# Block-sparse attention feeding a mixture of experts: the third chunk of keys is multiplied with V one step later, and the first group's queries alternate between the column halves of TensorE

## The chip, the core and the metric

The kernel runs on one core of one Trainium2 chip. The core has five engines with queues of their own: TensorE (PE, its weight loads are shown as PEld), VectorE (DVE), ScalarE (ACT), GpSimd (POOL) and SyncE (SP), which here issues most of the DMA transfers. Engines wait for one another through semaphores. Matrix products are written to PSUM banks, everything else lives in SBUF. The metric is the device time of one execution in microseconds (us).

## What is computed

The first half is BigBird attention: batch 4, 8 heads, 768 positions, head size 64, in blocks of 32 positions. A query block sees its own block and its two neighbours, the first and the last block, and three blocks drawn at random for it; the first and the last query block see everything. The second half is a mixture of 8 experts: a gate picks one expert for each of the 3072 rows, and the row goes through that expert's two layers.

```python
mask = np.abs(blk_i - blk_j) <= window
mask = mask | (blk_i == 0) | (blk_j == 0) | (blk_i == n_blocks - 1) | (blk_j == n_blocks - 1)
for qb in range(n_blocks):
    for kb in sampled_blocks[qb]:
        mask[qb * block:(qb + 1) * block, kb * block:(kb + 1) * block] = True
scores = np.where(mask, scores, -1000000000.0)
...
return np.matmul(attn, v).astype(np.float32)
...
x = np.ascontiguousarray(attn_out.transpose(0, 2, 1, 3)).reshape(B * S, H * D)
...
logits = x @ w_gate
expert_idx = np.argmax(logits, axis=1)
...
h = np.maximum(x_sorted[lo:hi] @ w1[e], 0.0)
y_sorted[lo:hi] = h @ w2[e]
return (gate_w[:, None] * y).astype(np.float32)
```

## The kernel before

**Steps.** Attention is a list of 48 steps, worked through by the loop over `steps` in the main program: 4 batches, in each 6 groups of queries, in each 2 halves (two pairs of heads, `pr`, a half). Step i has i % 12 as its place in the batch; even steps are a group's half 0, odd steps its half 1. A group is 128 queries in two tiles of 64 (`ti` 0 and 1). The first group of each batch (GL, places 0 and 1) is different: 64 ordinary queries, and the 64 queries of the first and the last block, which see all 768 keys.

**Keys and values.** An ordinary tile of queries has three chunks of 128 keys. For chunk 0 the rows of V are put in place by copies; for chunks 1 and 2 most of them are gathered from `v_rows` in DRAM by indirect DMAs on POOL (`fetch_values`, L525), four for a group, into `around`, which holds two groups. The gather for the second tile's chunk 2 is issued at the beginning of the group's own half 0, the other three during the group before. POOL's tiny copies into `paced` (`not_before`, L539) hold a gather back until another engine has got to a certain place.

**A step on each engine.** The order on all engines is written by hand. PE in step i: scores of step i (L349, L357), a transpose of 12 pieces of the next batch's K or Q (`turn`, L178; the staging tile is filled by SP, `fill_stage`, L140), in odd steps the transposes of a finished group (`turn_out`, L469), then the products with V of step i - 1 (`product`, L386), and in odd steps that finished group's gate logits (L492). ACT takes the exponentials of the scores (L362) into a ring of 7 tiles `ea`; DVE multiplies by the mask (L368, L372) and, when the products of step i - 1 are done, divides by the sums (`divide`, L445 to L451). When a group's half 1 is divided, SP stores its rows (L457). SP also loads V for the next batch (L161), writes it to `v_rows` (L170), and stores the gate weights (L517, L519). Each of SP's transfers is issued in the program's order.

**Halves of the array.** A product has 64 queries as columns of the stationary operand, so it uses one half of TensorE's columns, and its result lands in partitions 0 to 63 or 64 to 127 of a PSUM bank. `op[ti * D : (ti + 1) * D, ...]` in `product` picks the half by `ti`. Each product shows as two records in the trace, since the data is float32. An ordinary step has 24 products (48 records), tile 0 and tile 1 in turns. In the first group, `attend_last` takes 18 products for each pair: 12 that alternate between the halves, then 6 with `ti` 1 alone. In the first batch the 48 products of the 64 all-seeing queries are computed ahead of step 0 (`attend_all`), all with `ti` 1, and steps 1 and 2 then have 12 products each, all with `ti` 0.

**Banks.** The pool `ps_o` has two banks. One holds the results of one step; the logits are written beside them into the bank of step i - 1, and `divide` reads the bank and frees it.

**After attention** the experts run tile by tile: layer 1 (L1138), layer 2 (L1152). Their 2 MB weight transfers wait on SP for PE to free a buffer (L1085, L1088).

## Time and profile before

| what | value |
|---|---|
| median of three runs | 640.93 us (637.01 to 645.84) |
| the profiled execution | 638.06 us |
| its span, first to last instruction | 636.3 us |
| mean granted TensorE clock | 0.995 |
| attention (start to about 278.5) | 278.5 us |
| experts (278.5 to the end) | 357.8 us |
| PE / DVE / ACT / POOL busy | 96% / 50% / 36% / 30% |

The trace is of the profiled execution, and times in it count from its first instruction. A timeline row gives start, duration, engine, line, operation and operands, how many records are merged in it, and in brackets the idle time before it with what ended it. Matmuls overlap in the array, so a merged row of n records lasts n - 1 pitches and one full duration; a row that stops early shows where the engine had to wait.

### The profile page before, as it was taken

To read this page: it belongs to the slowest core of one execution; us is meant where nothing else is said; L and a number is where in the kernel's file an instruction comes from. 1 tells how busy PE (TensorE), PEld (TensorE's weight loads), DVE (VectorE), ACT (ScalarE), POOL (GpSimd) and SP (SyncE) were. 2 spreads that over 40 slices of the span, in tenths; PEclk is the share of its full clock that TensorE was granted. 3 is DMA by queue.
4 is the path that set the end of the run, shared out by engine and by line. 5 is a ranking of instruction groups with operands and counts; after the bars stand their busy time and mean duration, and the time that the engine had idled before them with its cause. 6 is when DMAs were issued, how large, how long until landed. Compare 5 with 4: busy or idle time off the path is not lost. (4 is left out here: it accounts for less than half of the span.)

```text
span 636.3 us, 20201 instructions
## 1 busy us (share of the span) xinstructions
PE 608.2 (96%) x8326; PEld 516.0 (81%) x8326; DVE 315.6 (50%) x1025; ACT 231.9 (36%) x456; POOL 193.8 (30%) x289
## 2 busy tenths in 40 slices
PE   6899999999999899999999999999999999999994
PEld 6888999998989899997777776877878787967862
DVE  7477767675778567635852485303190118203300
ACT  5376766665667577721111011111112111111110
POOL 2157745643456445720111221011401130020110
PEclk9899999999999999999999999999999999999999
DMA  8899966995696657899999999869998999769710
GB/s 264 207 193 246 288 162 153 255 261 154 136 247 206 184 147 250 261 322 369 338 305 313 344 388 336 303 229 379 396 399 281 365 399 399 291 205 407 299 40 20
DMA packets 125061, 170.86 MB, mean 269 GB/s; under 512 B 71236, under 2 KB 71237, under 8 KB 124934
## 3 DMA queue, kind: packets, MB, share of 16 engines
q1 hardware_dynamic: 114896, 137.61, 66.3%
q0 software_dynamic: 10000, 31.59, 16.0%
q8 instruction: 75, 1.23, 0.8%
q14 instruction: 52, 0.43, 0.2%
q10 hardware_dynamic: 38, 0.00, 0.0%
HBM read 150.11 MB, written 19.33 MB: 266 GB/s over the span
## 5 line engine op out<-in xcount | busy, mean ns | idle before, releaser
L525 POOL DMA_INDIRECT around<-v_rows,rows_of x88 | 100.0, 1136 | 55.3 <-DMA around<-v_rows 21.2
L362 ACT ACTIVATE ea<-s 128x768 f32<-128x768 f32 x104 | 83.6, 811 | 83.2 <-PE s L357 56.1
L1119 DVE STREAM_TRANSPOSE around<-xg 32x128 f32<-32x128 f32 x192 | 58.1, 303 | 86.9 <-DMA xg<-x_rows,gB 81.9
L1138 PEld LDWEIGHTS hp<-around,room 128*128 128x128 f32 x832 | 94.7, 192 | 3.9 <-issue 3.2
L1138 PE MATMUL hp<-around,room 128*128 128x128 f32 x832 | 96.8, 276 | 0.6 <-issue 0.3
L386 PE MATMUL op<-around,ea 128*64 128x65 f32 x2112 | 85.5, 224 | 8.8 <-DMA around<-v_rows,rows_of 5.1
L386 PEld LDWEIGHTS op<-around,ea 128*64 128x64 f32 x2112 | 75.4, 137 | 15.5 <-DMA around<-v_rows,rows_of 6.1
L368 DVE TENSOR_TENSOR ea<-ea,mask 128x768 f32<-128x768 f32 x80 | 74.6, 955 | 14.7 <-ACT ea L362 10.1
L1152 PE MATMUL zp<-room,kr 128*128 128x512 f32 x176 | 77.6, 594 | 0.0
L1145 ACT ACTIVATE kr<-hp 128x512 f32<-128x512 f32 x36 | 21.4, 597 | 116.0 <-PE hp L1138 98.3
L1172 POOL DMA_INDIRECT out_dram<-kr,sB x14 | 14.1, 1008 | 160.2 <-ACT kr L1162 97.9
L1152 PEld LDWEIGHTS zp<-room,kr 128*128 128x128 f32 x176 | 32.6, 190 | 37.2 <-issue 37.2
L357 PE MATMUL s<-other,kr 64*128 64x128 f32 x704 | 48.1, 272 | 0.3 <-issue 0.3
L357 PE MATMUL s<-room,kr 64*128 64x128 f32 x704 | 47.9, 272 | 0.2 <-issue 0.2
L1138 PEld LDWEIGHTS hp<-around,other 128*128 128x128 f32 x384 | 43.8, 192 | 2.3 <-issue 2.3
L1138 PE MATMUL hp<-around,other 128*128 128x128 f32 x384 | 44.3, 275 | 0.0
L357 PEld LDWEIGHTS s<-other,kr 64*128 64x128 f32 x704 | 43.7, 188 | 0.6 <-issue 0.6
L357 PEld LDWEIGHTS s<-room,kr 64*128 64x128 f32 x704 | 43.7, 188 | 0.0
L1250 DVE STREAM_TRANSPOSE ea<-ea 32x128 f32<-32x128 f32 x84 | 21.7, 285 | 30.9 <-DMA ea<-x_rows,gB 30.2
L1162 ACT ACTIVATE kr<-zp,xg 128x512 f32<-128x512 f32 x12 | 8.2, 687 | 74.9 <-PE zp L1152 74.9
L1152 PE MATMUL zp<-other,kr 128*128 128x512 f32 x80 | 35.3, 593 | 0.0
L1119 DVE STREAM_TRANSPOSE around<-kr 32x128 f32<-32x128 f32 x48 | 14.5, 302 | 36.3 <-PE hp L1138 34.9
(369 smaller groups left out, 831.2 us busy)
## 6 DMA issues: line engine op xcount, KB each, us to landing
room<-in_moe_w_dram SPq DMA_DIRECT2D x30, 2048.0 KB
other<-in_moe_w_dram SPq DMA_DIRECT2D x16, 2048.0 KB
room<-in_moe_w_dram SPq DMA_DIRECT2D x16, 512.0 KB
x_rows<-xb SPq DMA_DIRECT2D x20, 256.0 KB
room<-in_k_dram SPq DMA_DIRECT2D x24, 192.0 KB
room<-in_q_dram SPq DMA_DIRECT2D x24, 192.0 KB
v_rows<-room SPq DMA_DIRECT2D x12, 260.0 KB
v_rows<-other SPq DMA_DIRECT2D x12, 260.0 KB
```

Of the source, the lines that this page charges most:

```text
L357: nc.tensor.matmul(s[:, hh, a : a + P], lhsT=keys(r), rhs=moving, start=True, stop=True)
L362: nc.scalar.activation(e, s[:, :, : 6 * D], AF.Exp, scale=scale)
L368: nc.vector.tensor_tensor(e, e, m[:, None, :].to_broadcast([P, 2, 6 * D]), op=ALU.mult)
L386: nc.tensor.matmul(op[ti * D : (ti + 1) * D, pr % 2, hh, : D + 1], lhsT=e, rhs=values[:, (2 * pr + hh) * VW : (2 * pr + hh + 1) * VW], sta ...
L525: nc.gpsimd.indirect_dma_start(out=around[p0:, par, 1 + ti + 2 * ch, :], out_offset=None, in_=v_d[b][:, :], in_offset=bass.IndirectOffsetO ...
L1119: nc.vector.transpose(xT[d, :, t], xg[t, :DM].rearrange("p (c q) -> p c q", c=DB)[:, :, d])
L1138: nc.tensor.matmul(hp[:, m, :], lhsT=st[i]["w1"][:, c, fb * P : (fb + 1) * P], rhs=st[i]["xT"][:, c, :], start=(c == 0), stop=(c == DB - 1),)
L1145: nc.scalar.activation(hT[:, g * (FB // 2) : (g + 1) * (FB // 2), :], hp[:], AF.Relu)
L1152: nc.tensor.matmul(zp[:], lhsT=st[i]["hT"][:, fb, :], rhs=st[i]["w2"][:, fb, :], start=(fb == 0), stop=(fb == FB - 1),)
L1162: nc.scalar.activation(zo, zp[:], AF.Copy, scale=of_i)
L1172: ins = nc.gpsimd.indirect_dma_start(out=to[:, :], out_offset=bass.IndirectOffsetOnAxis(ap=at, axis=0), in_=rows, in_offset=None, bounds_c ...
L1250: nc.vector.transpose(xT_u[d, :, j * P + tq * 32 : j * P + (tq + 1) * 32], xg_u[t, j, :DM].rearrange("p (c q) -> p c q", c=DB)[:, :, d],)
```

## The change

Two things change in attention. First, for most ordinary steps (`in_two`: places 2 to 10 of a batch, 2 to 7 of the last) the products with chunk 2 are not done in step i + 1 with the others, but in step i + 2, ahead of the first two chunks of step i + 1. Each bank is thus written in two steps. A finished group's transposes and logits move from the odd step i + 2 to the even step i + 3 (i being the group's half 1); its logits are written beside the results of the older bank, which is divided behind them. In steps with no logits the older bank is divided at once. The gather of the first tile's chunk 2 stands behind the late products, and the pace of another gather hangs on the older bank's sums.

Second, in GL `side_of` swaps the two column halves for odd pairs of heads, and `in_turns` issues the products of one half and of the other alternately. Rows of `xb` then hold other queries for odd pairs, so SP stores a GL group with 6 transfers of 128-element pieces in place of 3 of whole rows, and the transposed logits' operand takes the other half.

```diff
+    def side_of(g, pr, ti):
+        return (ti + pr) % 2 if g == GL else ti
+
     def product(b, g, pr, ti, hh, e, values, last):
         bank, begun = bank_of(b, g, pr)
         op = bank[:, : 4 * (D + 4)].rearrange("p (r h w) -> p r h w", r=2, h=2)
+        side = side_of(g, pr, ti)
         nc.tensor.matmul(
-            op[ti * D : (ti + 1) * D, pr % 2, hh, : D + 1], lhsT=e, rhs=values[:, (2 * pr + hh) * VW : (2 * pr + hh + 1) * VW],
-            start=ti not in begun, stop=last, skip_group_check=True,
-        )
-        begun.add(ti)
+            op[side * D : (side + 1) * D, pr % 2, hh, : D + 1], lhsT=e, rhs=values[:, (2 * pr + hh) * VW : (2 * pr + hh + 1) * VW],
+            start=side not in begun, stop=last, skip_group_check=True,
+        )
+        begun.add(side)
+    def attend(units_, chunks):
+
+        for ch in chunks:
...
-    def attend_last(b, pr, e_all, e_two):
-        for ch in range(3):
-            for hh in range(2):
-                x = 3 * (pr % 2) + ch
-                product(b, GL, pr, 0, hh, e_two[:, hh, x * D : (x + 1) * D], values_of(b, GL, 0, ch), ch == 2)
-                if e_all is not None:
-                    product(b, GL, pr, 1, hh, e_all[:, hh, ch * D : (ch + 1) * D], sets[b][2][:, ch, :], False)
-        if e_all is not None:
-            attend_all(b, pr, e_all, range(3, NCH))
+    def of_all(b, pr, e):
+        return [
+            (b, GL, pr, 1, hh, e[:, hh, c * D : (c + 1) * D], sets[b][2][:, c, :], c == NCH - 1) for c in range(NCH) for hh in range(2)
+        ]
+
+    def of_last(b, pr, e):
+        return [
+            (b, GL, pr, 0, hh, e[:, hh, (3 * (pr % 2) + ch) * D : (3 * (pr % 2) + ch + 1) * D], values_of(b, GL, 0, ch), ch == 2)
+            for ch in range(3) for hh in range(2)
+        ]
+
+    def in_turns(*sides):
+        for two in zip(*sides, strict=True):
+            for one in two:
+                product(*one)
+
+    def attend_first(prs):
+        in_turns(*(of_all(0, pr, es[("all", pr)]) for pr in prs))
+
+    def attend_last(units_):
+        sides = [[], []]
+        for b, _, pr, _, e_two in units_:
+            sides[pr % 2] += of_last(b, pr, e_two)
+        for b, _, pr, e_all, _ in units_:
+            if e_all is not None:
+                sides[1 - pr % 2] += of_all(b, pr, e_all)
+        in_turns(*sides)
...
-    for pr in range(NPR):
-        attend_all(0, pr, es[("all", pr)], range(NCH))
+    for half in range(2):
+        attend_first((2 * half, 2 * half + 1))
...
-            for p, n, row in pieces(g):
-                nc.sync.dma_start(x_d[b * S + row : b * S + row + n, :DM], xb[p : p + n, :])
+            if g < GL:
+                for p, n, row in pieces(g):
+                    nc.sync.dma_start(x_d[b * S + row : b * S + row + n, :DM], xb[p : p + n, :])
+            else:
+                for a in range(2):
+                    for p, n, row in pieces(g):
+                        p = (p + a * D) % P
+                        nc.sync.dma_start(
+                            x_d[b * S + row : b * S + row + n, :DM].rearrange("n (r a w) -> n r a w", r=2, a=2)[:, :, a],
+                            xb[p : p + n, :].rearrange("n (r a w) -> n r a w", r=2, a=2)[:, :, a],
+                        )
...
-            lg = banks_of[beside][0][:, 4 * (D + 4) : 4 * (D + 4) + E]
+            lg = beside[:, 4 * (D + 4) : 4 * (D + 4) + E]
...
+                from_ = side_of(g, c, j)
                 nc.tensor.matmul(
-                    lg[j * D : (j + 1) * D, :], lhsT=xo[:, c * P + j * D : c * P + (j + 1) * D], rhs=wg[:, c, :],
+                    lg[j * D : (j + 1) * D, :], lhsT=xo[:, c * P + from_ * D : c * P + (from_ + 1) * D], rhs=wg[:, c, :],
...
+    def in_two(n):
+        return steps[n][1] != GL and n % (2 * NG) != 2 * NG - 1 and n < len(steps) - 4
+
+    out_at = {}
+    for n in range(1, len(steps) - 2, 2):
+        out_at[n + (3 if n < len(steps) - 4 else 2)] = steps[n][:2]
...
-        if half == 1 and i + 1 < len(steps):
-            not_before(mine[1][4][0:1, 0, 0:1])
-            fetch_values(*steps[i + 1][:2], 0, 1)
...
-        out_of = steps[i - 3][:2] if i >= 3 and half == 1 else None
+        units_of[i] = mine
+        out_of = out_at.get(i)
         if out_of:
             turn_out(*out_of)
         if copy_turned:
             copy_turned()
-        if i > 0 and before[0][1] != GL:
-            attend(before)
-        elif i > 0:
-            for b_, g_, pr, e_all, e in before:
-                attend_last(b_, pr, e_all, e)
+        closed = []
+        spare = None
+        if i > 1 and in_two(i - 2):
+            attend(units_of[i - 2], (2,))
+            closed.append(i - 2)
+            spare = banks_of[steps[i - 2]][0]
+            if not out_of:
+                divide(*steps[i - 2])
+        if half == 1 and i + 1 < len(steps):
+            not_before(mine[1][4][0:1, 0, 0:1])
+            fetch_values(*steps[i + 1][:2], 0, 1)
+        if i > 0:
+            if steps[i - 1][1] == GL:
+                attend_last(units_of[i - 1])
+            else:
+                attend(units_of[i - 1], (0, 1) if in_two(i - 1) else (0, 1, 2))
+            if not in_two(i - 1):
+                closed.append(i - 1)
+                spare = spare if spare is not None else banks_of[steps[i - 1]][0]
         if "gates" in rt:
             gate_weights()
         if out_of:
-            logits(*out_of, beside=steps[i - 1])
+            logits(*out_of, beside=spare)
             if out_of[1] == order[-1]:
                 gate(out_of[0])
-        if i > 0:
-            divide(*steps[i - 1])
+        for n in closed:
+            if steps[n] in banks_of:
+                divide(*steps[n])
...
-                b_, g_, half_ = steps[i - 1]
+                b_, g_, half_ = steps[closed[0]]
...
-    attend(before)
+    attend(units_of[i], range(3))
```

PE, batch 0, steps 4 and 5 before; `op_930` is the bank of step 3, `op_1050` that of step 4, `tp` the next batch's transposes, `xr` the finished group, and the last row the logits:

```order
L178 MATMUL tp_914<-ident_58,room_75 128x64 x12
L386 MATMUL op_930<-around_78,ea_77 64x65 x24
L357 MATMUL s_995<-room_75,xk_79 128x128 x2
...
L178 MATMUL tp_1023<-ident_58,room_75 128x64 x12
L469 MATMUL xr_1038<-ident_58,xb_850 128x64 x8
L386 MATMUL op_1050<-around_78,ea_77 64x65 x24
L492 MATMUL op_1050<-wg_63,xo_1047 64x8 x8
```

The same steps in the changed kernel; `op_805` is the bank of step 2, `op_919` that of step 3, `op_1042` that of step 4:

```order
L178 MATMUL tp_884<-ident_58,room_75 128x64 x12
L495 MATMUL xr_899<-ident_58,xb_646 128x64 x8
L390 MATMUL op_805<-around_78,ea_77 64x65 x8
L390 MATMUL op_919<-around_78,ea_77 64x65 x16
L519 MATMUL op_805<-wg_63,xo_908 64x8 x8
L357 MATMUL s_985<-room_75,xk_79 128x128 x2
...
L178 MATMUL tp_1011<-ident_58,room_75 128x64 x12
L390 MATMUL op_919<-around_78,ea_77 64x65 x8
L390 MATMUL op_1042<-around_78,ea_77 64x65 x16
```

The 24 products of a step are split 16 and 8 over two steps, and the transposes and logits stand in the even step; the number of instructions in a pair of steps is the same.

PE, step 13 (batch 1, GL), from the end of the scores through the products of the first pair of heads (those of the second follow in the same way) before; `around` is the 64 ordinary queries, `other` the all-seeing ones, x7 being one product that alternates and 6 alone:

```order
L357 MATMUL s<-other,kr 128x128 x4
L469 MATMUL xr<-ident,xb 128x64 x8
L386 MATMUL op<-around,ea 64x65
L386 MATMUL op<-other,ea 64x65
...
L386 MATMUL op<-other,ea 64x65 x7
...
L492 MATMUL op<-wg,xo 64x8 x8
```

The end of the scores and all products of that step in the changed kernel:

```order
L349 MATMUL s<-other 64x64 x48
L357 MATMUL s<-other,xk 128x128 x2
...
L390 MATMUL op<-around,ea 64x65 x12
L390 MATMUL op<-other,ea 64x65 x24
L357 MATMUL s<-other,xk 128x128 x2
```

Both pairs' ordinary products now come first, the first pair in one half and the second in the other, then the all-seeing ones of both likewise.

SP, batch 1, steps 12 to 17 before (`gw` gate weights of batch 0, `xb` attention rows, L161 V and L140 K and Q for batch 2):

```order
L161 DMA room<-in_v_dram 128x6x64 x4
L517 DMA x_rows<-gw 128x5x8
L519 DMA x_rows<-gw 64x8
L519 DMA x_rows<-gw 32x8 x2
L457 DMA x_rows<-xb 64x512
L457 DMA x_rows<-xb 32x512 x2
L161 DMA room<-in_v_dram 128x6x64 x4
L140 DMA room<-in_k_dram 128x6x64 x2
L457 DMA x_rows<-xb 128x512
L170 DMA v_rows<-room 128x520
L140 DMA room<-in_q_dram 128x6x64 x2
```

And changed:

```order
L161 DMA room<-in_v_dram 128x6x64 x4
L480 DMA x_rows<-xb 64x2x128
L480 DMA x_rows<-xb 32x2x128 x2
...
L161 DMA room<-in_v_dram 128x6x64 x2
L544 DMA x_rows<-gw 128x5x8
L546 DMA x_rows<-gw 64x8
L546 DMA x_rows<-gw 32x8 x2
L161 DMA room<-in_v_dram 128x6x64 x2
L140 DMA room<-in_k_dram 128x6x64 x2
L170 DMA v_rows<-room 128x520
L140 DMA room<-in_q_dram 128x6x64 x2
```

The gate weights go one step later and now stand behind the GL rows and ahead of the last V loads and the K fill; the rows of an ordinary group go one step later too, behind the next Q fill.

## Rows read from the trace of the kernel before

**Rows 1.** Busy time of each engine in stretches of the span: start and end, length, then busy us (instructions) of PE, PEld, DVE, ACT and POOL, granted clock, DMA share, GB/s. The first four are attention from step 2 on, the last the experts.

```profile
35.45:84.47 49.02, 47.55 (x1074) 45.87 (x1073) 36.63 (x101) 33.50 (x64) 33.18 (x66) 1.00 1.05 243
84.47:147.28 62.81, 60.79 (x1506) 58.49 (x1504) 43.32 (x130) 41.33 (x81) 31.56 (x51) 1.00 0.81 205
147.28:213.50 66.22, 62.25 (x1509) 59.40 (x1506) 47.64 (x156) 43.41 (x86) 33.02 (x44) 1.00 0.70 185
213.50:278.50 65.00, 61.94 (x1474) 58.33 (x1472) 39.89 (x114) 42.54 (x93) 34.65 (x45) 1.00 0.73 220
278.50:636.30 357.80, 348.46 (x2287) 268.93 (x2286) 127.27 (x461) 52.78 (x99) 52.25 (x54) 1.00 0.85 311
```

**Rows 2.** What PE waited for, the longest sums: us in total, times, longest.

```profile
PE op L386 <- DMA around<-v_rows,rows_of: 5.1, 7, 1.0
PE op L386 <- issue: 3.5, 7, 1.2
PE s L349 <- issue: 2.6, 5, 0.9
```

**Rows 3.** PE's timeline at the end of step 15, from its products to the first scores of step 16: a step that does not stop.

```profile
105.78 1.62 PE L386 MATMUL op<-around,ea 128*64 128x65 f32 x48
107.24 0.59 PE L492 MATMUL op<-wg,xo 128*64 128x8 f32 x16
107.76 0.49 PE L357 MATMUL s<-other,xk 64*128 64x128 f32 x4
```

**Rows 4.** The same stretch of step 17, to the first scores of step 18, and the products of step 18.

```profile
115.16 1.47 PE L386 MATMUL op<-around,ea 128*64 128x65 f32 x34
117.59 0.62 PE L386 MATMUL op<-around,ea 128*64 128x65 f32 x13 [0.97 <-DMA around<-v_rows,rows_of]
...
118.62 0.49 PE L357 MATMUL s<-other,xk 64*128 64x128 f32 x4
...
121.42 1.62 PE L386 MATMUL op<-around,ea 128*64 128x65 f32 x48
```

**Rows 5.** The same stretch, products to the next step's first scores, of steps 5, 7, 21, 29 and 35: the other steps whose products stop after 34 records.

```profile
52.42 1.27 PE L386 MATMUL op<-around,ea 128*64 128x65 f32 x34
...
55.76 0.49 PE L357 MATMUL s<-room,xk 64*128 64x128 f32 x4
...
63.16 1.26 PE L386 MATMUL op<-around,ea 128*64 128x65 f32 x34
...
65.81 0.49 PE L357 MATMUL s<-room,xk 64*128 64x128 f32 x4
...
135.92 1.27 PE L386 MATMUL op<-around,ea 128*64 128x65 f32 x34
...
138.62 0.49 PE L357 MATMUL s<-other,xk 64*128 64x128 f32 x4
...
180.50 1.27 PE L386 MATMUL op<-around,ea 128*64 128x65 f32 x34
...
183.69 0.49 PE L357 MATMUL s<-room,xk 64*128 64x128 f32 x4
...
210.48 1.26 PE L386 MATMUL op<-around,ea 128*64 128x65 f32 x34
...
213.50 0.84 PE L349 MATMUL s<-other 64*64 64x64 f32 x37
```

**Rows 6.** PE's timeline in step 13 and at the end of step 14: products of one column half alone.

```profile
94.25 0.81 PE L386 MATMUL op<-other,ea 128*64 128x65 f32 x11
...
95.60 0.86 PE L386 MATMUL op<-other,ea 128*64 128x65 f32 x12
```

**Rows 7.** PE's timeline from the products ahead of step 0 to those of step 2 (batch 0, one column half alone throughout).

```profile
20.44 2.84 PE L386 MATMUL op<-room,ea 128*64 128x65 f32 x26
24.50 4.30 PE L386 MATMUL op<-room,ea 128*64 128x65 f32 x70 [1.22 <-issue]
28.73 0.49 PE L357 MATMUL s<-room,xk 64*128 64x128 f32 x4
...
33.30 0.45 PE L386 MATMUL op<-around,ea 128*64 128x65 f32 x4 [1.13 <-DVE ea L372]
34.14 1.38 PE L386 MATMUL op<-around,ea 128*64 128x65 f32 x20 [0.39 <-DMA around<-v_rows,rows_of]
...
38.26 1.61 PE L386 MATMUL op<-around,ea 128*64 128x65 f32 x24
```

**Rows 8.** POOL's first gathers of V.

```profile
27.01 1.17 POOL L525 DMA_INDIRECT around<-v_rows,rows_of  x1 [21.21 <-DMA around<-v_rows]
28.49 0.93 POOL L525 DMA_INDIRECT around<-v_rows,rows_of  x1 [0.30 <-issue]
```

**Rows 9.** Stretches of the opening, columns as in rows 1.

```profile
16.00:20.00 4.00, 3.58 (x108) 3.34 (x112) 3.28 (x7) 2.35 (x5) 0.00 (x0) 0.90 0.89 240
20.00:22.00 2.00, 2.00 (x33) 1.88 (x28) 1.99 (x9) 0.81 (x1) 0.00 (x0) 0.50 1.20 318
22.00:24.00 2.00, 1.28 (x15) 1.08 (x13) 1.35 (x7) 1.55 (x6) 0.00 (x0) 0.85 0.64 213
```

**Rows 10.** DVE's timeline in step 31 (mask, logits, division), and PE's products in step 32.

```profile
192.80 1.82 DVE L368 TENSOR_TENSOR ea<-ea,mask 128x768 f32<-128x768 f32 x2
...
194.61 0.15 DVE L445 TENSOR_SCALAR sums<-op 128x4 f32<-128x4 f32 x1
...
195.01 0.42 DVE L451 TENSOR_TENSOR xb<-op,r 128x256 f32<-128x256 f32 x1
...
195.86 1.15 PE L386 MATMUL op<-around,ea 128*64 128x65 f32 x30
```

**Rows 11.** SP's timeline in batch 1 (steps 14 to 16), and the transposes on PE in step 18 that read what L140 brings.

```profile
103.13 0.37 SPq L517 DMA_DIRECT2D x_rows<-gw  x1
...
105.27 2.73 SPq L457 DMA_DIRECT2D x_rows<-xb  x3
108.04 2.36 SPq L161 DMA_DIRECT2D room<-in_v_dram  x4
110.50 2.79 SPq L140 DMA_DIRECT2D room<-in_k_dram  x2
...
120.96 0.54 PE L178 MATMUL tp<-ident,room 64*128 64x64 f32 x12
```

More of the change, by code (lines that the diff above doesn't have):

```diff
@@ L385, in product @@
         op = bank[:, : 4 * (D + 4)].rearrange("p (r h w) -> p r h w", r=2, h=2)
+        side = side_of(g, pr, ti)
         nc.tensor.matmul(
-            op[ti * D : (ti + 1) * D, pr % 2, hh, : D + 1], lhsT=e, rhs=values[:, (2 * pr + hh) * VW : (2 * pr + hh + 1) * VW],
-            start=ti not in begun, stop=last, skip_group_check=True,
-        )
-        begun.add(ti)
-    def attend(units_):
-        for ch in range(3):
+            op[side * D : (side + 1) * D, pr % 2, hh, : D + 1], lhsT=e, rhs=values[:, (2 * pr + hh) * VW : (2 * pr + hh + 1) * VW],
+            start=side not in begun, stop=last, skip_group_check=True,
+        )
+        begun.add(side)
+    def attend(units_, chunks):
+        for ch in chunks:
             for b, g, pr, _, e in units_:
@@ L399, in attend @@
                         product(b, g, pr, ti, hh, e[:, hh, x * D : (x + 1) * D], values_of(b, g, ti, ch), ch == 2)
-    def attend_all(b, pr, e, chunks):
-        for c in chunks:
-            for hh in range(2):
-                product(b, GL, pr, 1, hh, e[:, hh, c * D : (c + 1) * D], sets[b][2][:, c, :], c == NCH - 1)
-    def attend_last(b, pr, e_all, e_two):
-        for ch in range(3):
-            for hh in range(2):
-                x = 3 * (pr % 2) + ch
-                product(b, GL, pr, 0, hh, e_two[:, hh, x * D : (x + 1) * D], values_of(b, GL, 0, ch), ch == 2)
-                if e_all is not None:
-                    product(b, GL, pr, 1, hh, e_all[:, hh, ch * D : (ch + 1) * D], sets[b][2][:, ch, :], False)
-        if e_all is not None:
-            attend_all(b, pr, e_all, range(3, NCH))
+    def of_all(b, pr, e):
[21 more added lines that the diff above has]
+        in_turns(*sides)
     def turn_first(pr):
@@ L1321 @@
     steps = [(b, g, half) for b in range(B) for g in order for half in range(2)]
+    units_of = {}
+    def in_two(n):
[3 more added lines that the diff above has]
+        out_at[n + (3 if n < len(steps) - 4 else 2)] = steps[n][:2]
     for i, (b, g, half) in enumerate(steps):
@@ L1409 @@
             gather(i - len(steps) + 3)
-        before = mine
     turn_x(0)
-    attend(before)
+    attend(units_of[i], range(3))
     divide(*steps[-1])
```

## The prediction

> **What bounds the kernel now.** I read the busy time by stretches first, then PE's waits, then PE's timeline step by step. By stretches, PE is busy for nearly the whole of attention and of the experts (348.5 of 357.8 us there), while no other engine passes 75% of any stretch [rows 1]. So PE's own time and its stops are the span. Its waits are short: 5.1 us in 7 stops on gathered V, and 3.5 us in 7 stops of the products for which the profile names nothing [rows 2]. What a stop costs is longer than its idle time, since the row before it has not yet ended by the model when issuing stops; so I measure from a step's first product to the next step's first scores. Undisturbed, with logits, that is 107.76 - 105.78 = 1.98 us [rows 3]. In step 17 the products stop after 34 records, two into chunk 2, which starts at record 33: tile 1's chunk 2 has not landed. That stretch takes 118.62 - 115.16 = 3.46 us [rows 4].
>
> **Term 1, chunk 2 a step later.** Six odd steps stop after record 34: 5, 7, 17, 21, 29 and 35 [rows 4, 5]. Over 1.98 us they lose 1.36, 0.67, 1.48, 0.72, 1.21 and 1.04 us: 6.5 us together. One of them (step 7) has "issue" as its releaser in the trace; its place after record 34 is that of the others, so I count it. The change moves these eight products behind the next step's scores. In step 17 the gather has come at 117.59, and would then be wanted with the products of step 18, at 121.42 less the 1.48 us that are saved, 119.94: 2.3 us in hand [rows 4]. I take the whole 6.5 us; the bounds are 0 (the wait comes back elsewhere) and 6.5. The last such stop, in step 47, stays, as the last steps are not changed. What is late next would be chunk 1 (records 17 to 32), whose gathers are issued a group ahead; of the seven stops on gathered V only the opening's is at it.
>
> **Term 2, GL of batches 1 to 3.** A row of one half alone has 12 records in 0.86 us; with the last one's own 0.22 us taken off, 58 ns each [rows 6]. Where halves alternate, 48 records take 1.62 us: 30 ns each [rows 3]. Each GL step has 24 lone records (2 pairs of heads, 6 products, 2 records), which is 24 x 28 = 0.68 us, and there are 6 such steps: 4.1 us. The bound below is 0, if pairs of these shapes don't overlap; the bound above is 4.1. What hides nothing here: PE has no stop in those products.
>
> **Term 3, GL of batch 0.** Steps 1 and 2 have 24 lone records each. Step 2's take 1.61 us [rows 7], and would take 24 x 30 + 220 ns = 0.9: 0.7 us. In step 1, PE stands until a gather lands at 34.14 and then has 20 records, 1.38 us; changed, 8 records lie ahead of that stop and 16 behind it, 0.7 us: 0.7 us. Together 1.4 us.
>
> **Term 4, the opening, at nothing.** The 96 lone records ahead of step 0 last from 20.44 to 28.73 [rows 7]. Alternating would take up to 3.4 us from them: 70 x 28 ns = 2.0, and 26 records at 108 ns, twice the lone pitch, would give 1.4. But the next stop but one is the gather at 34.14, and POOL issues the first gathers at 27.01 and 28.49, when earlier DMAs have landed, not PE [rows 8]. PE comes to that stop earlier and waits longer. Bounds 0 and 3.4; I take 0, as the gather's row is the nearest.
>
> **What is moved at no cost.** Transposes and logits of a finished group go from odd to even steps, and the number of instructions in a pair of steps stays. On DVE the division of the older bank has a new deadline: it frees the bank in which the next step's first chunks begin. In step 31 the mask ends at 194.62 and the products of step 32 begin at 195.86, 1.2 us later; a division behind the mask takes 0.8 us (194.61 to 195.43), while PE first has 16 records of the older bank, 0.5 us [rows 10]. So 0.9 us are in hand in this, one of the tightest steps. The ring `ea` holds three steps of two tiles and has 7. On POOL the gather behind the late products waits for the mask of the same step anyway, so nothing behind it is later. On SP, GL's store is 6 transfers for 3: 3 took 2.73 us to issue [rows 11], so up to 2.7 us a batch, beside work that waits for nothing there. The exception is batch 1: V and K of batch 2 stand behind this and behind the gate weights, now a step later. The K fill is issued until 113.29 and read by PE at 120.96, 7.7 us later [rows 11]. The change takes 1.5 us of that (PE's own saving) and some 1.2 us (the later issue). I charge 0.5 us, between 0 (landed early) and 2.7 (it lands just in time now).
>
> **Sum.** 6.5 + 4.1 + 1.4 - 0.5 = 11.5 us. The experts keep their length, since PE frees the buffers that their weights go into. The profiled execution took 638.06 us, so 626.6. That execution lies 2.9 us under the median of 640.93; the stops vary from run to run, and without them runs should lie closer together, so I forecast **627 us**, 2.2% under the median.
>
> **Rivals.**
>
> *The clock falls in the opening (chance 0.22).* Around 20 us the granted clock fell to half: 0.90 in 16 to 20, 0.50 in 20 to 22, 0.85 in 22 to 24, 3.4 us at 1.2 GHz in all, after a stretch in which PE was busy for 3.58 of 4 us [rows 9]. Changed, PE would be through with the first scores at about 29 (33.30 less its idle 1.13, less 3.4) and stand until 34, 5 us instead of 1.13 + 0.39 [rows 7]. A fall of the same length just behind it costs 3.4 / 2 = 1.7 us: 628.3. Against it: the two idle times that are there now left the clock at full speed. The Trainium skill, "TensorE: Matmul & The Clock Gate", section "HAM oscillation — how this bites in real kernels", says that a wait for DMA between bursts of matmuls puts the clock back to half; by that rule this case would be the likely one, and no row here shows such a fall after a single wait.
>
> *Only the packing pays (0.18).* Transfers are the true pace of batches 0 and 1 (DMA share 1.05 and 0.81 [rows 1]), and PE that comes earlier meets them at the transposes of K and Q or at chunk 1. Then terms 2 and 3 remain: 638.06 - 5.5 = 632.6. Against it: the transposes in rows 11 have no idle time before them.
>
> *The alternation isn't one (0.05).* If the halves don't overlap in GL's order, 638.06 - 6.5 + 0.5 = 632.1. Against it: rows 3 show just this alternation; for it, only that the two operands now come from different tiles of exponentials.
>
> *Slower: PE waits for the bank (0.07).* Place: the first product of each of the 33 moved steps, which needs the division of the older bank, behind masks and logits on DVE. If DVE comes later than the 0.9 us that step 31 leaves, PE stops there. It decides at 12 / 33 = 0.36 us a step: with 0.5 us each the kernel is at 626.6 + 16.5 = 643. For it: batches 2 and 3 put routing work behind DVE's divisions. Against it: step 31 is one of those. The Trainium skill, "TensorEngine Tiling (Array Packing)", section "PSUM Bottleneck", warns that tiling speeds up TensorE and not the emptying of PSUM, which may become the limit; that speaks for this rival, and the trace so far shows no products waiting for a division.
>
> **How the numbers follow.** The forecast has 0.48, its own range being 624 to 630. The range runs from 621 (the opening's 3.4 us gained too, and terms 1 to 3 in full: 638.06 - 12.0 - 3.4 = 622.7, less some 1.5 us for stops of other kinds) to 636 (packing only, on the median's scale: 632.6 + 2.9). It leaves out the slower case and little else. A measurement can tell about 2%, so under 628.1 counts as faster by more than that. That holds for about two thirds of the forecast's chance (0.34), half of the clock's (0.11) and a little of the packing case: 0.47 faster, 0.50 within 2%, 0.03 slower, as even the bank case lies mostly within 2%.
>
> **What would show it.** Right: no products stopping behind a gather in steps 5, 7, 17, 21, 29 and 35; GL steps' products 2.3 us instead of 3.0; the wait at 34 us longer, at the same time of the span; experts 357 to 358 us. Wrong: stops at L178 around step 18, granted clock of 0.5 after 34 us, products waiting for DVE's xb, or the first gathers of V landing earlier.

## The result, and the profile after

The changed kernel takes **646.1 us** (median of 20 runs, 641.9 to 651.6), the kernel before 640.35 in the runs beside them. The ratio is 1.0095, 95% interval 1.0073 to 1.0117: about 1% slower, less than the 2% up to which I said that a measurement tells no change. The longest of the 20 runs was in a slower state of the chip and is not in the ratio. I had said 627, and 621 to 636; the time lies outside. The profiled execution took 647.34 us (before: 638.06), its span is 645.6 us, its mean granted clock 0.975 (before: 0.995).

First, the same five stretches as [rows 1], cut at the same places of the program (first scores of steps 2, 12, 24 and 36, first expert matmul). Columns as there.

```profile
32.58:83.44 50.86, 46.96 (x1036) 45.28 (x1032) 36.01 (x99) 34.20 (x67) 38.32 (x62) 0.97 1.04 235
83.44:147.05 63.61, 60.47 (x1508) 57.44 (x1504) 42.82 (x131) 41.38 (x80) 33.84 (x55) 1.00 0.85 206
147.05:216.15 69.10, 62.69 (x1511) 59.36 (x1507) 47.96 (x157) 41.63 (x83) 31.13 (x44) 0.98 0.68 173
216.15:287.61 71.46, 65.25 (x1516) 61.29 (x1513) 42.19 (x118) 44.33 (x97) 34.78 (x46) 0.95 0.71 220
287.61:645.60 357.99, 348.62 (x2286) 268.93 (x2286) 127.27 (x461) 52.80 (x99) 52.26 (x54) 0.99 0.85 308
```

The experts are as long as before (357.99 against 357.80 us). Step 2 starts 2.87 us earlier (32.58 against 35.45), step 12 only 1.03 earlier, and each of the three stretches behind is longer: by 0.8, 2.9 and 6.5 us.

PE's waits from 28 to 290 us, as in [rows 2]:

```profile
PE tp L178 <- DMA room<-in_k_dram: 6.1, 5, 2.1
PE op L390 <- issue: 4.5, 13, 0.5
PE s L357 <- issue: 3.3, 4, 2.3
PE s L349 <- issue: 2.5, 3, 1.7
```

The 5.1 us on gathered V have gone from this execution. In their place stand 6.1 us at L178, the transposes of the next batch's K and Q (all five stops are at a K), which [rows 11] show without idle time. Two more executions of this kernel, after_again and after_third, have 4.4 and 1.4 us of waits on V, in steps 1 and 45, and none in the six steps that the change was made for; at L178 they have 7.2 and 3.4 us. Two of the five stops at L178, the first with the products behind it, from PE's timeline:

```profile
54.84 0.59 PE L178 MATMUL tp<-ident,room 64*128 64x64 f32 x12 [2.14 <-DMA room<-in_k_dram]
55.24 0.44 PE L495 MATMUL xr<-ident,xb 64*128 64x64 f32 x8
55.61 1.62 PE L390 MATMUL op<-around,ea 128*64 128x65 f32 x48
...
66.19 0.59 PE L178 MATMUL tp<-ident,room 64*128 64x64 f32 x12 [1.76 <-DMA room<-in_k_dram]
```

Now the end of attention: step 46 takes 8.69 us, 4.01 in the kernel before, whose products and next scores are the first two rows here:

```profile
268.72 1.65 PE L386 MATMUL op<-around,ea 128*64 128x65 f32 x48
270.30 0.49 PE L357 MATMUL s<-other,xk 64*128 64x128 f32 x4
...
269.72 0.49 PE L357 MATMUL s<-other,xk 64*128 64x128 f32 x4
...
272.40 0.45 PE L390 MATMUL op<-around,ea 128*64 128x65 f32 x7
273.15 0.34 PE L390 MATMUL op<-around,ea 128*64 128x65 f32 x4 [0.30 <-issue]
273.91 0.39 PE L390 MATMUL op<-around,ea 128*64 128x65 f32 x5 [0.42 <-issue]
274.66 0.39 PE L390 MATMUL op<-around,ea 128*64 128x65 f32 x5 [0.37 <-issue]
275.41 0.34 PE L390 MATMUL op<-around,ea 128*64 128x65 f32 x4 [0.36 <-issue]
276.15 1.46 PE L390 MATMUL op<-around,ea 128*64 128x65 f32 x22 [0.41 <-issue]
...
278.41 0.80 PE L357 MATMUL s<-other,xk 64*128 64x128 f32 x4
```

The profile names no wait for the 48 products after the change, yet their records come four or five at a time, every 0.75 us. The last row's 0.80 us for four records that take 0.49 at 269.72 is half clock. The granted clock (the number before the DMA share) around three stops:

```profile
64.00:67.50 3.50, 1.74 (x46) 1.51 (x46) 2.25 (x5) 0.98 (x2) 3.25 (x6) 1.00 0.76 191
67.50:71.00 3.50, 3.50 (x62) 3.48 (x58) 0.81 (x4) 1.98 (x5) 0.37 (x2) 0.51 1.08 302
...
190.50:193.90 3.40, 1.05 (x22) 0.97 (x19) 2.45 (x13) 0.45 (x2) 0.78 (x2) 1.00 1.16 300
193.90:197.30 3.40, 3.40 (x55) 3.17 (x55) 2.88 (x10) 2.88 (x6) 2.35 (x4) 0.50 0.70 140
...
272.00:275.80 3.80, 2.29 (x38) 1.58 (x36) 0.96 (x1) 0.85 (x2) 2.95 (x3) 1.00 0.96 301
275.80:282.60 6.80, 6.45 (x77) 6.41 (x78) 2.52 (x6) 1.84 (x3) 0.00 (x0) 0.50 0.63 234
```

Each time PE stands for part of the first stretch (it is busy for 1.74, 1.05 and 2.29 us) and goes at 1.2 GHz in the next one: 3.4 + 3.4 + 6.8 = 13.6 us, in stretches where [rows 1] have 1.00.

### The profile page after: what moved, and what is told of

Same layout as the page of the kernel before. It is cut to its first block, busy times and chain, and to the rows that moved or that the text cites. A ratio compares the mean times of both kernels' runs of the same rounds, so it can differ in the third digit from the quotient of the medians.

```text
span 645.6 us, 20213 instructions
## 1 busy us (share of the span) xinstructions
PE 611.6 (95%) x8326; PEld 517.8 (80%) x8326; DVE 316.4 (49%) x1025; ACT 231.6 (36%) x456; POOL 198.1 (31%) x289
## 5 line engine op out<-in xcount | busy, mean ns | idle before, releaser
L390 PE MATMUL op<-around,ea 128*64 128x65 f32 x2112 | 79.3, 229 | 5.3 <-issue 4.5
L390 PEld LDWEIGHTS op<-around,ea 128*64 128x64 f32 x2112 | 70.6, 141 | 11.3 <-issue 6.6
L357 PE MATMUL s<-room,kr 64*128 64x128 f32 x704 | 49.6, 274 | 3.3 <-issue 3.0
L357 PE MATMUL s<-other,kr 64*128 64x128 f32 x704 | 49.5, 278 | 0.0
L357 PEld LDWEIGHTS s<-room,kr 64*128 64x128 f32 x704 | 45.2, 189 | 4.0 <-issue 3.6
L357 PEld LDWEIGHTS s<-other,kr 64*128 64x128 f32 x704 | 45.6, 194 | 0.0
```

The source lines that it names most:

```text
L357: nc.tensor.matmul(s[:, hh, a : a + P], lhsT=keys(r), rhs=moving, start=True, stop=True)
L390: nc.tensor.matmul(op[side * D : (side + 1) * D, pr % 2, hh, : D + 1], lhsT=e, rhs=values[:, (2 * pr + hh) * VW : (2 * pr + hh + 1) * VW], ...
```

## The experiments

Theories: **A**, TensorE, let off its stops on V, meets the fills of K and Q; **B**, new stops cost again through the clock; **C**, the store of x, a step later, holds SP's weight parts back, and these make step 46 long; **D**, batch 0 goes at the pace of its transfers; **E**, POOL's first gather of expert rows makes step 46 long. Each ratio is to runs of the kernel before beside it on the same chip, since chips differ: before takes about 640 us on all but one of them, and 630 on that one.

One table first, to be looked up as each kernel comes. It has the profiled executions on the chips where before takes 640 us, cut at PE's first scores of steps 13, 25, 36 and 47 (before: 90.18, 153.07, 213.50, 270.30), as us more (+) or less than before's.

| kernel | to 13 | 13 to 25 | 25 to 36 | 36 to 47 | rest | sum |
|---|---|---|---|---|---|---|
| before, us | 90.18 | 62.89 | 60.43 | 56.80 | 366.0 | 636.3 |
| predicted | -3.4 | -3.1 | -3.6 | -1.4 | 0 | -11.5 |
| changed | +0.4 | +0.6 | +1.8 | +5.5 | +1.2 | +9.3 |
| after_third (changed) | +0.2 | -0.1 | -2.5 | +5.9 | -0.7 | +2.8 |
| late_alone | -0.1 | +2.0 | -0.8 | +5.5 | +0.9 | +7.4 |
| halves_alone | +0.4 | -2.2 | +2.5 | -1.0 | +1.3 | +0.9 |
| fills_early | +1.8 | -0.3 | -3.3 | +5.0 | -1.0 | +2.2 |
| opening_old | +2.1 | -0.1 | -1.1 | +4.9 | -0.7 | +5.1 |
| before_fills | 0.0 | +0.8 | -0.3 | +0.2 | +0.4 | +1.1 |
| late_012_no_halves | -1.0 | +2.1 | -1.5 | +1.5 | +0.4 | +1.5 |
| best_again | -0.3 | -0.3 | -3.1 | 0.0 | +1.5 | -2.3 |
| parts_early_again | +1.2 | +1.3 | -0.7 | +7.0 | -0.8 | +8.0 |
| gather_later | +0.8 | +0.4 | -2.2 | +6.2 | +1.0 | +6.1 |

Two executions of one kernel differ by 4.3 us in one stretch (changed and after_third, 25 to 36), so only what several rows share is read from it.

### The two parts, each alone

late_alone has the third chunk late, with the halves, the opening and GL's store of before; halves_alone the reverse, by this edit of the changed kernel:

```diff
-        return steps[n][1] != GL and n % (2 * NG) != 2 * NG - 1 and n < len(steps) - 4
+        return False
...
-        out_at[n + (3 if n < len(steps) - 4 else 2)] = steps[n][:2]
+        out_at[n + 2] = steps[n][:2]
```

> The third chunk a step later and nothing else: queries keep their halves in a first group, the opening and the store of x are those of before. Theory A (the fills of K and Q are the next thing that TensorE meets): the 6.1 us of stops behind the gathered V are gone, stops at the turns of K and Q of 3 to 6 us stand in their place in batches 0 and 1, and the time is 638 to 642, no better than before. Theory B (each of the new stops costs again through the granted clock): the mean clock is under 0.985 and the time 641 to 645. Theory of the prediction (the term is real, and it is the halves that lose): 632 to 635.

> The halves from pair to pair alone: all three chunks stay in the step behind their scores. Products of the six first-group steps behind batch 0 at 2.32 us instead of 3.02, of the opening at some 3.3 us for 96. Theory A: what is won meets the gathered V, whose stops grow from 6.1 us to 8 or more, and the time is 638 to 641. Theory B: hardly a new stop, so the clock stays at 0.99 and the time is 635 to 638. If the halves are what loses (their store of x in six pieces, or the opening): 643 or more.

late_alone: 643.61 us, 1.0046 (1.0015 to 1.0077); mean clock of its runs 0.985. halves_alone: 640.35 us, 1.0007 (0.9974 to 1.0041); stops on gathered V 7.1 us in 8. So the late chunk is what loses, and the halves alone gain nothing that can be measured. For late_alone A misses by both its numbers: the time lies over 638 to 642, and the stops at L178 are 2.0 us and not 3 to 6. B has the time, and the clock is just over its limit. In halves_alone the waits on V are short of A's 8; before, they are 5.1 us in this document's profile (not the 6.1 that both expectations put there) and 9.2 in before_again's, so their growth isn't shown.

### The fills of K and Q

```diff
-                if 4 <= here < 8:
-                    fill_next(b + 1, here)
+                if 3 <= here < 7:
+                    fill_next(b + 1, here + 1)
```

> The changed kernel with the fills 4 to 7 of K and Q in each batch issued a step earlier, in steps 3 to 6 of the batch. Theory A: the stops at the turns of K and Q (6.1 us) fall under 3 us, and the time by 3 to 6, to 640 to 643. If the transfers of batch 0 are together the pace (busy share 1.01 in both kernels between 28 and 90 us), the stops only change their place, to V or the keep of V, and the time stays at 645 to 647. Theory B: the time follows the mean clock: over 0.985 gives 643 or less, under 0.98 646 or more, wherever the stops are.

> The kernel before with fills 4 to 7 a step earlier, and nothing of the change. Theory A (the fills became the wait only because the third chunk no longer held TensorE back): no gain, a ratio of 0.998 to 1.002. If the early fills are a gain by themselves, that the change only happened to need: 0.993 to 0.997.

fills_early (on the changed kernel): 641.0 us, 1.0007 (0.9973 to 1.0041), within A's numbers; its one stop at L178 is 0.3 us:

```profile
PE tp L178 <- DMA room<-in_q_dram: 0.3, 1, 0.3
```

Its mean clock over 12 runs is 0.981, that of the changed kernel 0.980: the time fell with the clock as it was, against B. before_fills (the same edit on the kernel before): 640.4 us, 1.0013 (0.998 to 1.0046), nothing. The fills became a wait only with the late chunk; with them issued earlier the ratio is 0.4 to 0.9% lower (1.0007 beside the changed kernel's 1.0051 and 1.0095; the intervals of the first two overlap, and two more pairs below go the same way).

### The opening in the old order

```diff
-    for half in range(2):
-        attend_first((2 * half, 2 * half + 1))
+    for pr in range(NPR):
+        attend_first((pr,))
```

> The changed kernel with the opening's 96 products pair after pair, one half of the columns at a time, as before. The 96 products take some 4.7 us or more instead of 3.3. Theory A: the first steps are 1 to 3 us later and the stops in steps 6 and 8 shrink by as much, so that from step 9 on nothing differs: 645 to 647. If the half clock between 9.6 and 23 us belongs to the packed opening, the clock there is 0.9 and more as before and the time 2 to 5 us lower.

642.54 us, 1.0022 (0.9986 to 1.0059): not longer than the changed kernel, and under A's 645 to 647. Half clock from 9.3 to 22.9 us is there with either order, and in another execution of the kernel before too (9.9 to 23.6), so it is not the packing's. A later one goes with the packing: in ten of the twelve profiled executions with the packed opening the granted clock falls to 0.50 at 31.7 to 34.4 us, for 3.4 us or more, in or behind a stop of step 1's products, and in one (late_alone) of the eight with the old order. The changed kernel's profile above and after_third's are the two without it; after_again has it:

```profile
33.08 0.69 PE L390 MATMUL op<-around,ea 128*64 128x65 f32 x16 [2.77 <-DMA around<-v_rows,rows_of]
...
30.00:34.20 4.20, 1.43 (x32) 1.22 (x32) 1.71 (x7) 1.73 (x5) 2.80 (x4) 1.00 1.22 201
34.20:37.60 3.40, 3.40 (x36) 3.40 (x36) 2.70 (x8) 0.81 (x1) 1.15 (x2) 0.50 1.21 220
```

What it costs by itself was not measured. The table's first column agrees with **D**: all twelve executions come to step 13 at 89.2 to 92.3 us, none of them 3.4 us ahead of before as terms 1 and 3 have it, whatever PE saves in the opening or in batch 0, where DMA's share is 1.05 before [rows 1] and 1.04 after. That the transfers are the reason is argued from that share; no run made them shorter.

### The last batch

late_012 keeps batch 3 in the old order (with early fills), late_012_fills_old the same without them, late_12 leaves batch 0 in the old order too:

```diff
-        return steps[n][1] != GL and n % (2 * NG) != 2 * NG - 1 and n < len(steps) - 4
+        return steps[n][1] != GL and n % (2 * NG) != 2 * NG - 1 and n < len(steps) - 2 * NG
...
-        out_at[n + (3 if n < len(steps) - 4 else 2)] = steps[n][:2]
+        out_at[n + (3 if n < len(steps) - 2 * NG else 2)] = steps[n][:2]
```

parts_early issues an even step's weight parts a step earlier, both_early has the early fills too:

```diff
-        for what in PARTS.get(late, ()):
-            fetch_part(*what)
+        for n in (late,) if late < 11 else (late, late + 1) if late % 2 else ():
+            for what in PARTS.get(n, ()):
+                fetch_part(*what)
```

> The changed kernel with the weight parts of each even step from step 12 of the last batch's count on issued a step earlier, so that they stand ahead of the store of x in SP's order, as they do in the kernel before. Theory C (the store of x, now a step later, holds the weight parts behind it on SP, and the two parts that so reach step 46 slow its products): step 46 falls from 8.7 us to 5 or less and the time by 3 to 5, to 641 to 643. If the parts are not the cause, step 46 stays at 8 to 9 us and the time at 645 to 647.

> Fills 4 to 7 of K and Q and the weight parts a step earlier, both. Theories A and C together: stops at the turns of K and Q under 3 us, step 46 at 5 us or less, and 636 to 638, 1 to 2 per cent under the changed kernel and a little under before. If only A holds: 640 to 642, as with the fills alone.

> The changed kernel with the early fills, and with the third chunk a step later in batches 0 to 2 only: batch 3 keeps the order of before. Against the early fills alone (641.0): if what the late chunk costs lies in batch 3, batch 3 (step 36 to the end of step 46) falls from some 55 us to 50 or 51 and the time to 636 to 638. If batch 3 is as long as before, nothing there belongs to the late chunk.

> The changed kernel again, unchanged, so that it stands on the same chip as the three beside it. Theory C (weight parts behind the later store of x): step 46 takes 8 us or more again, against 4 to 4.7 in the kernels whose parts stand ahead. Theory A: stops at the turns of K and Q of 4 to 7 us. Ratio to before 1.006 to 1.012. If the ratio is under 1.003 here, the loss belonged to one chip, and nothing more is to be explained.

> The changed kernel with the third chunk late in batches 0 to 2 alone, and nothing else: fills where the change has them, weight parts ahead of the store of x in batch 3 by the old order. Theory C alone: 4 to 5 us under the changed kernel of the same call, a ratio of 1.000 to 1.003 to before. Theory A then has the rest: stops at the turns of 4 to 6 us stay. If C is wrong, it is as long as the changed kernel.

> The third chunk late in batches 1 and 2 alone, the early fills, the packed opening. Theory D (batch 0 goes at the pace of its transfers, busy share 1.0, so that nothing TensorE saves there counts): the same as with batch 0 late too, a ratio of 0.993 to 0.999. If the late chunk of batch 0 is worth its share of the prediction (three stops, 2.5 us): 0.4 per cent longer.

These kernels ran on the chip where before takes 630 us. There the changed kernel (after_again) is at 1.0031 (0.9995 to 1.0068), with 7.2 us of stops at L178, and its step 46 takes 4.64 us with the parts where the change puts them: that says nothing for C. From step 36 to step 47 it is 2.6 us over before_again (55.84 against 53.27), but so, nearly, are kernels with the old order there: the three with the late order in batch 3 take 55.0 to 55.8 us on this chip, the five without 53.3 to 55.6. parts_early: 1.0015 (0.9983 to 1.0047); both_early: 0.9974 (0.9939 to 1.0009); late_012: 0.9957 (0.9923 to 0.9991); late_012_fills_old: 1.0014 (0.9978 to 1.0049); late_12: 0.9968 (0.9933 to 1.0003). On this chip it is the early fills that go with a ratio below 1: 1.0015 to 0.9974 and 1.0014 to 0.9957, each pair one edit apart. late_12 beside late_012 agrees with D (batch 0's late chunk is worth nothing either way), but the intervals would also hold the 0.4% of the other theory.

Back on chips with 640 us:

> The changed kernel, a third time. If the long step 46 belongs to a chip: 8 to 9 us where the time of before is about 640, 4 to 5 us where it is about 630. If it belongs to the change alone, it comes and goes between runs of one chip. Ratio to before 1.003 to 1.010; stops at the turns of K and Q 5 to 8 us on either.

> The changed kernel with each even step's weight parts a step earlier on SP, again, now for step 46 alone, since the chip of its first run showed no long step 46 in any kernel. Theory C (the two parts of step 46 stand behind the later store of x and so start in the middle of it): where the time of before is about 640, step 46 is 4 to 5 us instead of 7.4 to 8.7, and the time 3 to 4 us under the changed kernel. If it is 7 or more on such a chip, C has fallen. Where the time of before is about 630, nothing is told apart.

> The changed kernel with POOL's first gather of expert rows, which stands at the end of step 45, moved to the end of step 46, behind the last gather of V. Theory E (that gather and the weight parts run in step 46 together, and the gather is what slows the products): step 46 at 4 to 5 us where before takes about 640. Theory C: step 46 stays at 7 us or more. On a chip with before at 630: 4 to 5 us by both.

after_third: 643.1 us, 1.0051 (1.0023 to 1.0078), step 46 7.37 us. parts_early_again: 645.48 us, 1.0108 (1.0068 to 1.0147), step 46 8.56 us; gather_later, whose one edit puts POOL's gather of the first expert rows a step later in the program, 645.5 us, 1.0118 (1.0061 to 1.0175), step 46 8.15 us.

```diff
-        if i >= len(steps) - 3:
-            if i == len(steps) - 1:
-                not_before(mine[1][4][0:1, 0, 0:1])
-            gather(i - len(steps) + 3)
+        if i == len(steps) - 2:
+            gather(0)
+        if i == len(steps) - 1:
+            gather(1)
+            not_before(mine[1][4][0:1, 0, 0:1])
+            gather(2)
```

**C falls.** In parts_early_again the parts are issued by 264.18, 6.3 us ahead of step 46 (270.50 to 279.06), SP issues nothing else in that step, and the step takes 8.56 us. **E isn't settled by gather_later**: the edit moves the gather in the program, but POOL issues it in step 46 all the same, at 270.25, where that step lasts from 267.28 to 275.43:

```profile
270.25 0.95 POOL L1083 DMA_INDIRECT xg<-x_rows,gA  x1 [0.30 <-issue]
271.50 0.95 POOL L1083 DMA_INDIRECT xg<-x_rows,gA  x1 [0.30 <-issue]
...
269.96 0.39 PE L390 MATMUL op<-around,ea 128*64 128x65 f32 x5
270.52 0.36 PE L390 MATMUL op<-around,ea 128*64 128x65 f32 x4 [0.17 <-issue]
```

Against E is that the first stop, ahead of 270.52, comes while POOL is still issuing it.

What the table shows is that the late order in batch 3 itself goes with +4.9 to +7.0 us from step 36 to step 47 in all seven executions that have it, and that the five without it have -1.0 to +1.5. Step 46 takes 7.4 to 8.8 us in the seven and 4.0 to 4.1 in the others, where the transposes and logits that moved into it account for 0.6 us (4.64 in after_again); so 3.4 to 4.8 us of the loss lie in this step. One more thing differs there, and no run moved it by itself: the store of x is issued from 1.1 us before to 0.7 us after step 46's first scores in the seven, and 3.5 us before them in the five (on the 630 us chip it stands as late, without the stops). In the best kernel:

```profile
264.89 1.70 PE L390 MATMUL op<-around,ea 128*64 128x65 f32 x48
266.52 0.49 PE L357 MATMUL s<-other,xk 64*128 64x128 f32 x4
```

### The best version, what the halves are worth in it, and the kernel before beside itself

late_012_open_old, run again as best_again: early fills, third chunk late in batches 0 to 2, the opening in the old order, halves from pair to pair. late_012_no_halves is the same without the halves.

> The third chunk late in batches 0 to 2, the early fills, and the opening's products in the old order. If the packed opening is worth nothing, since the next product waits for gathered V in either order (rows of four kernels: 0.6 us where it is packed late, 3.4 to 4.4 where it is early), this is within 0.3 per cent of the same kernel with the packed opening, a ratio of 0.993 to 0.999. If the opening's 1.4 us are real: 1 to 2 us longer.

> The same kernel as late_012_open_old, again: third chunk late in batches 0 to 2, early fills, opening's products in the old order, halves from pair to pair. Ratio to before 0.990 to 0.996, the same mean clock as the changed kernel or a little more, stops at the turns of K and Q under 3 us.

> Third chunk late in batches 0 to 2, early fills, opening in the old order, and queries that keep their halves in a first group. Beside best_again, which has the halves from pair to pair as its one difference: if the halves are worth their 4.1 us, this one is 0.5 to 0.7 per cent longer, a ratio of 0.998 to 1.000. If the first-group steps end at another wait whichever way the halves lie, the two are within 0.2 per cent.

625.42 us, 0.9927 (0.9899 to 0.9955) on the 630 us chip; 636.88 us, 0.996 (0.9935 to 0.9985) on a 640 us chip: faster than the kernel before by 0.4 to 0.7%, well under 2%, and than the changed kernel by 1.0% (625.42 / 631.41 and 636.88 / 643.1). A stop of 2.07 us at a K fill is left in the first of the two profiles. Without the halves 640.23 us, 0.9981 (0.9948 to 1.0013). By the medians the halves are worth 3.4 us here, by the ratios 1.3, and the intervals overlap.

> The kernel before, unchanged, for the granted clock of each of its runs. Theory B (the changed kernel is longer because it is at half clock more often): its mean clock over the runs is 0.99 or more, against 0.980 of the changed kernel, and its time falls by about 3 us for each 0.01 of clock, as the changed kernel's does. If its mean clock is 0.985 or less, the clock explains at most half of the 6 us.

627.95 us, 0.9972 (0.9948 to 0.9996), mean clock 0.988, between the two values that were to decide on B: the kernel before beside itself. Ratios within some 0.3% of 1, the changed kernel's 1.0031 on this chip among them, are therefore not told from 1.

## Why the prediction was wrong, point by point

**Term 1 (6.5 us): the stops went, the time did not.** In the changed kernel's profile not one product waits on gathered V [rows 4, 5 against the waits after], and in no execution of it does one in the six steps. The step that failed is the one that took "the whole 6.5 us": its lower bound, 0, said "the wait comes back elsewhere", and it does. In batch 0 it comes back at the K fills (2.14 and 1.76 us); in batch 1 late_alone and late_012_no_halves are 2 us longer than before, where term 1 has 2.2 us less. Of these 4.2 us three stops at L178 are 2.0 in late_alone: 0.42, 0.40 and 1.16 us, for which the trace names issue, the K fill and ACT's exponentials, so the early fills alone can't take all of it away (late_012_no_halves, with early fills, stops there for ACT's exponentials too, 1.56 us). The other 2 us are not accounted for. I had gone one row ahead ("7.7 us later") for one fill of batch 1, and not at batch 0's, where SP issues V and K alternately.

**The sum had no term for batch 3.** I counted six stops to be removed and no cost of the late order where there was none to remove. It is the largest single loss where before takes 640 us, +4.9 to +7.0 us, and its place is shown; its cause isn't.

**Term 2 (4.1 us) was right in size, term 3 too, and both were mostly hidden.** PE's products of the GL step 12, in step 13, and the next scores:

```profile
94.78 0.92 PE L390 MATMUL op<-around,ea 128*64 128x65 f32 x24
95.53 1.57 PE L390 MATMUL op<-other,ea 128*64 128x65 f32 x48
...
97.03 0.49 PE L357 MATMUL s<-other,xk 64*128 64x128 f32 x4
```

From 94.78 to the end of the 48 at 97.10 are 2.32 us, where before's took 3.0. Steps 1 and 2 take 0.92 us for 24 records, as said. That the halves don't overlap (the rival at 0.05) is refuted. In halves_alone the 13 to 25 stretch is 2.2 us shorter, and batch 2 gives it back.

**Term 4 (the opening, at nothing) was right, and its reason too.** The 96 products take 3.30 us here; before's took from 20.44 to the next scores at 28.73, with a stop of 1.22 us and part of it at half clock, and before_again's 6.21 us in one row. POOL's first gather is issued at 25.00 us instead of 27.01, but it waits for a DMA as before, and in all twenty profiled executions, of either order, it comes between 25.0 and 27.1 (before_again 26.23, after_third 26.28): not PE, as I had said.

```profile
22.58 3.30 PE L390 MATMUL op<-room,ea 128*64 128x65 f32 x96
...
25.00 1.17 POOL L552 DMA_INDIRECT around<-v_rows,rows_of  x1 [19.21 <-DMA around<-v_rows]
...
31.73 0.92 PE L390 MATMUL op<-around,ea 128*64 128x65 f32 x24 [0.61 <-DVE ea L372]
```

In all six executions with the packed opening on the 630 us chip PE "comes to that stop earlier and waits longer", 2.8 to 4.4 us (2.77 in after_again); in the profile here it does not wait there. Of the 2.87 us by which step 2 is early here, 0.35 are left at step 9 (70.01 against 70.36) and none at step 13.

**"Nothing behind it is later" on POOL was wrong.** The tiny copy that paces a gather hangs on the older bank's sums, and these come a step's logits later. What POOL waits for there has doubled, and ACT, whose exponentials need a tile that POOL's copy has still to read, waits behind it (the last two rows are before's):

```profile
POOL paced L566 <- DVE sums L462: 55.6, 27, 4.7
...
ACT ea L362 <- POOL paced L566: 7.6, 6, 1.8
...
POOL paced L539 <- DVE sums L445: 27.0, 19, 4.8
...
ACT ea L362 <- POOL paced L539: 2.4, 2, 1.2
```

The first is 50.1 us in after_third and 41.8 in after_again, the second 5.0 and nothing. How much of it reaches PE was not tried.

**The rivals.** "Transfers are the true pace of batches 0 and 1" (0.18) was the nearest: batch 0 agrees with it, and so does where PE meets them, "the transposes of K and Q"; the gain it left, 5.5 us, did not come either. The clock (0.22) was put into the opening, at 1.7 us, behind the longer stop there; after_again has just that, the changed kernel's own profile does not. There it fell behind later stops: 13.6 us at half speed, at most 6.8 us of time, but nowhere from 28 us to the end of attention in after_third's, which is still 2.8 us over before. Over the runs, the changed kernel's time goes by 3.3 us for 0.01 of mean clock (20 runs; 2.9 without the longest), and its clock is 0.980 where before's is 0.986: some 2 of the 6 us, if the one follows from the other. The rule of the Trainium skill that I weighed there, a return to half clock after a wait for DMA between bursts ("TensorE: Matmul & The Clock Gate", "HAM oscillation — how this bites in real kernels"), agrees with the stop at 64 to 66 us and what follows it. For the stops ahead of the other two falls the trace names no DMA. The slower rival, PE waiting for the bank, did not happen: no product waits for a division, and the 0.9 us in hand were enough. So the side was wrong by a mechanism that I had not priced on that side.

**Chances and signs.** Of the four signs named against the forecast, three came: stops at L178, clock at 0.5 behind 34 us, earlier first gathers (which other executions show without the change). Of the four for it, three came too: no stops in the six steps, 2.3 us in a first group, experts of 358 us; the wait at 34 us was not longer here. So each of the signs for it could come true without the gain.

## What to carry to other kernels

Before a wait is counted as gained, move the engine forward by that much against each of its other inputs: here the next one (K and Q) had less in hand than the sum took, and issuing it a step earlier took back 0.4 to 0.9%. Expect little back from a stretch whose DMA share is 1.0 when an engine gets faster in it: here batch 0, at 1.04, gave nothing. Make a reordering only in the steps where there is a stop to remove: in the last batch it had little to win, and lost 5 us where before takes 640. Before a difference between two profiles is put down to the edit, look for it in another execution of each kernel: the first gather's 2 us were not the change's.

## What the runs showed of the hardware that was not expected

In step 46 of the changed kernel's profile TensorE gets four or five records every 0.75 us at a granted clock of 1.00, with no wait named, and ACT's exponential in the same step stands 2.95 us, its releaser given only as remote:

```profile
271.68 0.81 ACT L362 ACTIVATE ea<-s 128x768 f32<-128x768 f32 x1 [1.66 <-PE s L357]
275.44 0.81 ACT L362 ACTIVATE ea<-s 128x768 f32<-128x768 f32 x1 [2.95 <-remote]
```

Six kernels with the late order in batch 3 have stops without a named wait in that step on the chips with 640 us (in after_third they are at its scores and transposes), and on the chip with 630 the changed kernel does not (its 48 products take 1.62 us). The weight parts don't make it; whether the gather of expert rows or the store of x does is open. And the same change is worth a different amount on different chips: 1.0031 where before takes 630 us, 1.0051 and 1.0095 where it takes 640.
